# Pooled attention with a PReLU feed-forward net: the low bits of the weight words by ScalarE, pooling of two chunks by TensorE, a reordered first phase

## The chip, the cores and the metric

The kernel runs on one core of a Trainium2 chip. Its time is the device time of one execution in microseconds (us). Three timed runs of the kernel before gave a median of 908.95 us (908.25 to 910.93). The profile is of one more execution.

## The reference

```python
# attention: B, H, S, D = 8, 8, 576, 64, pool = 8; q and k carry a factor 8
k_p = k.reshape(B, H, S // 8, 8, D).mean(axis=3)
v_p = v.reshape(B, H, S // 8, 8, D).mean(axis=3)
scores = matmul(q, k_p.T) / sqrt(D)
attn = exp(scores - max(scores));  attn = attn / (sum(attn) + 1e-9)
x = matmul(attn, v_p)              # heads side by side: 4608 tokens x 512
# feed-forward: w_in 512 x 2048, w_out 2048 x 512, alpha per column of h
h = x @ w_in
g = maximum(h, 0) + alpha * minimum(h, 0)
out = g @ w_out
```

The two weight matrices arrive as words of 8 bytes (float64), everything else as float32.

## The kernel before

The 4608 tokens go in nine chunks of 512. A chunk needs the pooled keys and values of one or two batches, its scores, a softmax, the mixing product (`mix`, L543), and then the two feed-forward products: FFN1 (L671 to L673) in 16 steps of 128 columns of h, FFN2 (L717 to L719) in 16 steps that add one block of g each to the outputs of four token blocks. Every product runs in float16 pairs: a value is split into a high half and the rest, and each product is three matmuls (low by high, high by low, high by high). A FFN step for 512 tokens is so 12 matmuls. The splits need powers of two as scales, from maxima over partitions: `reduce_max` (L168 to L193) transposes the column of maxima on TensorE (L189), takes the maximum of each row on VectorE (L181), spreads it over a diagonal on VectorE (L182), sums the diagonal into all partitions on TensorE (L191) and clamps it on VectorE (L186).

The work has two phases. `start()` (L730 to L801) does chunk 0 wholly, the attention of chunk 1, and turns the weights into float16 pairs. A loop (L819 to L836) then goes over chunks 1 to 8 and lays the attention of the next chunk between the FFN1 steps of this one. The loop's text is the same before and after, except that it hands over the first chunk's g blocks by number instead of in a list.

The weight tiles are 128 partitions x 2 x 512 words: eight of w_in, eight of w_out. `convert` (L569 to L622) takes such a tile as pairs of 32-bit integers, `word(l, i, 1)` the high and `word(l, i, 0)` the low half of each word. ScalarE scales the high words as if they were float32 (L577 in two halves for w_in, L581 for w_out), which brings the exponent to the float32 place; VectorE shifts that left by three bits (L585), puts the top three bits of the low words under it (L587: shift right by 29, or), and puts the sign on (L590). ScalarE rounds to float16 (L601, L606), and the rest goes to VectorE or POOL: for w_in L620, every second tile on POOL, for w_out L609 on VectorE in 15 of 16 halves and otherwise L613 on ScalarE with L615 on POOL. Before all this VectorE takes the maxima of the raw tile (L210).

What waits for the weights: an FFN1 step needs its w_in block and x; its result is scaled out of PSUM by ScalarE (L677), goes through PReLU on VectorE (L681), is rounded by ScalarE (L688), and its rest is made by POOL (L691). An FFN2 step needs g, its w_out block, and, in `start()`, that all of FFN1 be scaled out, since its four accumulators (`acc`) take the PSUM of both. Idle stretches of TensorE are filled with matmuls whose result is not used (L739), in the first chunk only.

Keys and values of `start()` come in a transposed layout: k as 128 x 2304 (eight tokens of a window side by side), v as 72 x 4096. For chunk 0 VectorE sums the keys' windows (L308). For chunk 1 POOL does it in three halving steps (L303). POOL does the same for both chunks' values (L402). q is scaled to float16 by ScalarE (L370) and its rest made by VectorE (L382); one half of chunk 1's q goes over ScalarE and POOL instead (L376, L378).

The order of `start()` is worked out by a list scheduler when the kernel is built (`_Plan`, L61 to L115). Each operation carries an engine, an assumed cost, its predecessors, a rank, and buffers that it takes or gives. The scheduler goes forward in its own model time and lets each engine take, of the operations that are ready at about the same time, the one with the lowest rank. What results is a fixed instruction order for each engine: an engine executes its row in order, whatever is ready elsewhere. DMAs are issued by SyncE in such a row of its own.

## Time and profile before

| | us |
|---|---|
| median of three runs | 908.95 |
| the profiled execution | 907.43 |
| its span in the trace | 905.7 |
| TensorE busy in the span | 853.0 |
| VectorE busy | 447.2 |
| ScalarE busy | 398.0 |
| POOL busy | 394.0 |
| first FFN1 matmul of chunk 0 | at 56.11 |
| last conversion of a weight on VectorE ends | at 177.8 |
| first FFN1 matmul of chunk 1 | at 190.60 |

The span runs from the first to the last instruction that the trace holds; the profiled execution is 1.73 us longer. All times of a row are counted from the span's start. The granted TensorE clock was 0.975 of full speed in the mean. The stretch up to 190.6 us is `start()`, the rest the loop over chunks 1 to 8.

### The profile page before, as it was taken

To read this page: it belongs to the slowest core of one execution; us is meant where nothing else is said; L and a number is where in the kernel's file an instruction comes from. 1 tells how busy PE (TensorE), PEld (TensorE's weight loads), DVE (VectorE), ACT (ScalarE), POOL (GpSimd) and SP (SyncE) were. 2 spreads that over 40 slices of the span, in tenths; PEclk is the share of its full clock that TensorE was granted. 3 is DMA by queue.
4 is the path that set the end of the run, shared out by engine and by line. 5 is a ranking of instruction groups with operands and counts; after the bars stand their busy time and mean duration, and the time that the engine had idled before them with its cause. 6 is when DMAs were issued, how large, how long until landed. Compare 5 with 4: busy or idle time off the path is not lost.

```text
span 905.7 us, 11601 instructions
## 1 busy us (share of the span) xinstructions
PE 853.0 (94%) x4494; PEld 416.9 (46%) x4494; DVE 447.2 (49%) x733; ACT 398.0 (44%) x659; POOL 394.0 (43%) x386
## 2 busy tenths in 40 slices
PE   6587877889999999999999999999999999999998
PEld 5343343445444544454444444544454445444443
DVE  6999999746513651375137613641474136211110
ACT  3665565455632563256225522552354336323330
POOL 5539727635722572257125723471356027302320
PEclk8699998999999999999999999999999999999999
DMA  9791311550541054105410531063106102200000
GB/s 309 237 351 48 122 33 45 99 195 4 92 150 50 4 95 148 49 4 98 155 38 4 120 134 39 4 132 121 38 4 134 42 12 47 47 35 13 1 20 27
DMA packets 93015, 74.75 MB, mean 83 GB/s; under 512 B 77024, under 2 KB 77600, under 8 KB 92960
## 3 DMA queue, kind: packets, MB, share of 16 engines
q1 hardware_dynamic: 92960, 74.01, 29.0%
q8 instruction: 35, 0.57, 0.3%
q14 instruction: 20, 0.16, 0.1%
HBM read 45.10 MB, written 9.44 MB: 60 GB/s over the span
## 4 chain that ended last, share of the span: by engine, by line
PE 75%; DVE 15%; POOL 3%; DMA 2%; issue 2%; ACT 2%; SPq 1%; POOLq 0%; ACTq 0%; DVEq 0%
PE o L717 12%; PE o L719 12%; PE o L718 12%; PE h L671 11%; PE h L672 11%; PE h L673 11%; DVE v L587 2%; DVE v L590 2%; DVE m L210 2%; DMA qraw<-qT_dram 2%; DVE t L681 2%; DVE w L609 1%; PE x L543 1%; DVE v L585 1%; PE s L533 1%
## 5 line engine op out<-in xcount | busy, mean ns | idle before, releaser
L691 POOL TENSOR_TENSOR g<-t,g 128x512 f16<-128x512 f32 x144 | 178.9, 1246 | 312.5 <-ACT g L688 312.5
L681 DVE SCALAR_TENSOR_TENSOR t<-t,al 128x512 f32<-128x512 f32 x144 | 140.5, 976 | 251.0 <-ACT t L677 240.4
L671 PE MATMUL h<-x,w 128*128 128x512 f16 x576 | 219.8, 382 | 10.9 <-ACT t L677 8.1
L672 PE MATMUL h<-x,w 128*128 128x512 f16 x576 | 219.7, 381 | 1.2 <-DVE x L504 1.2
L673 PE MATMUL h<-x,w 128*128 128x512 f16 x576 | 219.3, 381 | 0.0
L718 PE MATMUL o<-w,g 128*128 128x512 f16 x544 | 207.1, 381 | 0.0
L717 PE MATMUL o<-w,g 128*128 128x512 f16 x544 | 205.9, 381 | 1.2 <-ACT o L707 1.2
L719 PE MATMUL o<-w,g 128*128 128x512 f16 x544 | 204.1, 381 | 0.0
L688 ACT CAST g<-t 128x512 f16<-128x512 f32 x144 | 88.7, 616 | 126.3 <-DVE t L681 126.0
L677 ACT ACTIVATE t<-h,rp 128x512 f32<-128x512 f32 x144 | 98.3, 683 | 84.8 <-PE h L673 79.1
L402 POOL TENSOR_TENSOR vraw<-vraw 72x512 f32<-72x512 f32 (+1 forms) x64 | 66.8, 1059 | 87.1 <-DMA vraw<-vT_dram 80.0
L672 PEld LDWEIGHTS <-w 128*128 128x128 f16 x576 | 56.6, 98 | 75.9 <-issue 14.0
L719 PEld LDWEIGHTS <-g 128*128 128x128 f16 x576 | 56.6, 98 | 69.0 <-issue 1.9
L673 PEld LDWEIGHTS <-w 128*128 128x128 f16 x576 | 56.6, 98 | 68.7 <-issue 3.1
L717 PEld LDWEIGHTS <-g 128*128 128x128 f16 x576 | 56.6, 98 | 68.5 <-issue 3.2
L718 PEld LDWEIGHTS <-g 128*128 128x128 f16 x576 | 56.7, 98 | 67.2 <-issue 2.6
L707 ACT ACTIVATE o<-o,os 128x512 f32<-128x512 f32 x34 | 22.6, 683 | 146.6 <-PE o L719 146.6
L671 PEld LDWEIGHTS <-w 128*128 128x128 f16 x576 | 56.6, 98 | 65.8 <-issue 2.0
L471 POOL TENSOR_TENSOR e<-e,sm 128x576 f32<-128x576 f32 x35 | 43.6, 1245 | 40.6 <-DVE sm L469 40.5
L504 DVE SCALAR_TENSOR_TENSOR x<-x,xsc,x 128x512 f16<-128x512 f32 x36 | 25.9, 747 | 70.1 <-ACT x L500 70.1
L476 ACT CAST apad<-e 128x576 f16<-128x576 f32 x72 | 44.9, 668 | 14.8 <-POOL e L471 13.9
L479 POOL TENSOR_TENSOR apad<-e,apad 128x448 f16<-128x448 f32 x36 | 42.9, 1191 | 13.9 <-ACT apad L476 13.9
(126 smaller groups left out, 849.9 us busy)
## 6 DMA issues: line engine op xcount, KB each, us to landing
w<-w_dram SPq DMA_DIRECT2D x16, 1024.0 KB
vraw<-vT_dram SPq DMA_DIRECT2D x32, 288.0 KB
out_dram<-o SPq DMA_DIRECT2D x36, 256.0 KB
qraw<-qT_dram SPq DMA_DIRECT2D x17, 512.0 KB
kraw<-kT_dram SPq DMA_DIRECT2D x14, 576.0 KB
kq<-kT_dram SPq DMA_DIRECT2D x2, 576.0 KB
aT<-apad SPq DMA_TRANSPOSE x36
kq<-qT_dram SPq DMA_DIRECT2D x1, 512.0 KB
```

The lines of the kernel that those rows point to most:

```text
L402: nc.gpsimd.tensor_tensor(out=o, in0=y, in1=z, op=ALU.add)
L476: x = add("ACT", 0.57, lambda l=l, ap=ap, ev_=ev_: nc.scalar.copy(out=ap[:, l, :, :SP], in_=ev_()), x, *td[i - 2:i - 1], rank=rk)
L671: nc.tensor.matmul(ps, w[:, 1, ks_], x[:, 0], start=(n == 0), stop=False)
L672: nc.tensor.matmul(ps, w[:, 0, ks_], x[:, 1], start=False, stop=False)
L673: nc.tensor.matmul(ps, w[:, 0, ks_], x[:, 0], start=False, stop=(n == NK - 1))
L677: nc.scalar.activation(t, hps.pop((c, f)), AF.Copy, scale=rp[:, f:f + 1])
L681: nc.vector.scalar_tensor_tensor(out=t, in0=t, scalar=al[:, f:f + 1], in1=t, op0=ALU.mult, op1=ALU.max)
L688: nc.scalar.copy(out=g[:, 0], in_=t)
L691: nc.gpsimd.tensor_tensor(out=g[:, 1], in0=t, in1=g[:, 0], op=ALU.subtract)
L717: nc.tensor.matmul(ps, g[:, 1, ts_], w[:, 0], start=(f == 0), stop=False)
L718: nc.tensor.matmul(ps, g[:, 0, ts_], w[:, 1], start=False, stop=False)
L719: nc.tensor.matmul(ps, g[:, 0, ts_], w[:, 0], start=False, stop=(f == NF - 1))
```

## The change

- The low words become small integers on ScalarE: in place, from unsigned 32-bit through a scale of 0.9365 x 2^-29 to a signed integer of 0 to 7 (L614 after). VectorE then shifts the scaled high word left by three and ors the small integer in one instruction (L628 after), and puts the sign on (L631 after). The shift of its own (L585) is gone, so a tile has two VectorE steps in place of three.
- Keys and values of chunks 0 and 1 arrive in their natural layout, 576 tokens by 512 (new inputs kN, vN), and TensorE pools them by a product with a window matrix of ones (`pooled`, L273 and L276 after, float32, five blocks of tokens; 20 matmuls for the keys, five for the values). ScalarE copies the result out of PSUM. L308, L402 and L303 are gone from `start()`. The rest of chunk 1's q is made by VectorE wholly.
- In `reduce_max` the diagonal moves from VectorE to ScalarE (L202 after).
- Of the 16 halves of w_out, ten instead of 15 have their rest made by VectorE; the other six go over ScalarE and POOL.
- The scheduler has other costs and ranks (`RK`), the maxima and the diagonal are operations of their own, and an FFN2 step may come as soon as all of FFN1 is scaled out, in any order that the ranks give.

```diff
+LOW3 = 0.9365 * 2.0 ** -29
...
+RK = dict(l1=257.15, step=3.65, l2=347.18, mx1=499.67, mx1s=-14.75, mx2=209.79, mx2s=20.58, grp=17.42,
...
-    HOP, DMA_HOP = 0.08, 2.0
+    HOP, DMA_HOP = 0.12, 2.0
...
+    pool = const.tile([P, SP + 4 * P // POOL], F32, name="pool")
+    nc.vector.memset(pool, 0.0)
+    w0 = 4 * P // POOL
+    nc.vector.memset(pool[:, w0:w0 + P // POOL], 1.0)
+    for k, b in ((1, 0), (-1, POOL - 1)):
+        nc.gpsimd.affine_select(out=pool[:, w0:w0 + P // POOL], in_=pool[:, w0:w0 + P // POOL], compare_op=ALU.is_ge,
+                                fill=0.0, base=b, pattern=[[-k * POOL, P // POOL]], channel_multiplier=k)
...
+        def maxima():
+            nc.vector.tensor_reduce(out=t()[:n], in_=ps()[:n, 0, :P], axis=AX.X, op=ALU.max)
+
         def diagonal():
-            nc.vector.tensor_reduce(out=t()[:n], in_=ps()[:n, 0, :P], axis=AX.X, op=ALU.max)
-            nc.vector.tensor_scalar(out=dg()[:n, :n], in0=ident[:n, :n], scalar1=t()[:n], scalar2=None, op0=ALU.mult)
+            nc.scalar.activation(dg()[:n, :n], ident[:n, :n], AF.Copy, scale=t()[:n])
...
-        x = add("DVE", 0.5, diagonal, x, rank=rank)
-        x = add("PE", 0.35, lambda: nc.tensor.matmul(ps()[:, 1, :n], ones[:n], dg()[:n, :n], start=True, stop=True),
+        x = add("DVE", 0.27, maxima, x, rank=rank)
+        x = add("ACT", 0.28, diagonal, x, rank=rank)
+        x = add("PE", 0.45, lambda: nc.tensor.matmul(ps()[:, 1, :n], ones[:n], dg()[:n, :n], start=True, stop=True),
...
+    def pooled(add, src, dst, rank, by_rows, behind=(), place=None):
+        t = place or big_tile([P, 4, DM], "nat")
+        u = once(lambda: fp.tile([P, DM], F32, tag="f", name="nat4"))
+        ps = once(lambda: ps_s.tile([P, 2, CH], F32, tag="s", name="pl"))
+        lds = []
+        for j in range(2):
+            lds += 2 * [load(add, lambda j=j: t()[:, 2 * j:2 * j + 2],
+                             src[2 * j * P:(2 * j + 2) * P].rearrange("(a p) n -> p a n", p=P), 1.6, rank,
+                             *behind, *lds[-1:], take=None if j else "aT" if place else "big")]
+        lds.append(load(add, lambda: u()[:S - 4 * P], src[4 * P:], 0.4, rank, lds[-1], take="f"))
+        def products(j):
+            rows, n = (t()[:, j], P) if j < 4 else (u(), S - 4 * P)
+            win = pool[:n, w0 - P // POOL * j:w0 - P // POOL * j + SP]
+            if by_rows:
+                nc.tensor.matmul(ps()[:SP, 0], win, rows[:n], start=(j == 0), stop=(j == 4))
+                return
+            for pp in range(NPR):
+                nc.tensor.matmul(ps()[:, 0, pp * SP:pp * SP + SP], rows[:n, pp * P:pp * P + P], win,
+                                 start=(j == 0 and pp == 0), stop=(j == 4 and pp == NPR - 1))
+        x = None
+        for j, ld in enumerate(lds):
+            x = add("PE", 0.95 if by_rows else 1.5, lambda j=j: products(j), ld, *([x] if x else []), rank=rank,
+                    take=None if j else "S", give=None if j < 4 else "f" if place else ("f", "big"))
+        if by_rows:
+            x = add("ACT", 0.69, lambda: nc.scalar.copy(
+                out=dst().rearrange("p h d -> p (h d)"), in_=ps()[:SP, 0]), x, rank=rank, take="f", give="S")
+        else:
+            x = add("ACT", 0.5, lambda: nc.scalar.copy(
+                out=dst().rearrange("p a s -> p (a s)"), in_=ps()[:, 0, :NPR * SP]), x, rank=rank, take="f", give="S")
+        return x, lds[0]
...
+                place = (lambda: qk()[:, 1].rearrange("p (a n) -> p a n", n=DM)) if early else None
+                kl[b] = pooled(add, kN[b], ks, rank, False, behind, place)
+                continue
...
-                if i < q_pool:
-                    h = add("ACT", 0.2 + 0.84 / q_cuts, lambda t=t, sc=sc, cs=cs: nc.scalar.activation(
-                        t()[:, :, cs], t()[:, :, cs], AF.Copy, scale=sc()), h, rank=rk)
-                    h = add("Pool", 0.1 + 2.0 / q_cuts, lambda q=q, t=t, cs=cs: nc.gpsimd.tensor_tensor(
-                        out=q()[:, 1, :, cs], in0=t()[:, :, cs], in1=q()[:, 0, :, cs], op=ALU.subtract),
-                        h, *h_after, rank=rk, **kw)
...
-            ps = []
+            ps = [pooled(add, vN[b], vs, rank + rks["v"], True, behind)[0]] if begin else []
...
+            low = add("ACT", 1.2, lambda: nc.scalar.activation(
+                word(l, i, 0).bitcast(I32), word(l, i, 0).bitcast(U32), AF.Copy, scale=LOW3), w_ld[l, i],
+                      rank=rank + RK[f"low{l}"])
...
-            x = add("DVE", 0.6, lambda: nc.vector.tensor_scalar(
-                out=vi(), in0=vi(), scalar1=3, scalar2=None, op0=ALU.logical_shift_left), x, rank=rank)
-            x = add("DVE", 1.13, lambda: nc.vector.scalar_tensor_tensor(
-                out=vi(), in0=word(l, i, 0).bitcast(I32), scalar=29, in1=vi(),
-                op0=ALU.logical_shift_right, op1=ALU.bitwise_or), x, rank=rank)
-            x = add("DVE", 1.13, lambda: nc.vector.scalar_tensor_tensor(
+            x = add("DVE", 1.3, lambda: nc.vector.scalar_tensor_tensor(
+                out=vi(), in0=vi(), scalar=3, in1=word(l, i, 0).bitcast(I32),
+                op0=ALU.logical_shift_left, op1=ALU.bitwise_or), x, low, rank=rank)
+            x = add("DVE", 1.4, lambda: nc.vector.scalar_tensor_tensor(
                 out=vi(), in0=word(l, i, 1).bitcast(I32), scalar=-2 ** 31, in1=vi(),
...
-                if picked(2 * i + j, 15):
-                    ys.append(add("DVE", 0.6, lambda j=j, sf=sf: nc.vector.scalar_tensor_tensor(
...
-        x = rd[-1]
+        x = rd
...
-            x = add("PE", 2.59, lambda f=f: step(f), gd[f], wd[2, f], x, rank=due[2](f))
-        attention(add, 1, [1], L2 + 0.62, early=True, k_pool=2, q_pool=1,
-                  on_act=(0, 1), behind=[ld[2, NF // 2 - 1]])
+            x = [add("PE", 2.59, lambda f=f: step(f), gd[f], wd[2, f], *x, rank=due[2](f))]
+        attention(add, 1, [1], L2 + RK["a1"], begin=True, on_act=(0, 1), behind=[ld[2, NF // 2 - 1]])
```

The first place is VectorE while it converts w_out, behind the middle of FFN1. `v` is the tile under conversion, `w` the raw tile with its number, `s` the scales, `t` an FFN1 result, `pt`, `pm`, `pr`, `e`, `wsc`, `w2s` and `w2e` the small tiles of a reduction or of the scales. Before:

```order
L587 SCALAR_TENSOR_TENSOR v<-w_629,v 128x1024
L585 TENSOR_SCALAR v<-v 128x1024
L590 SCALAR_TENSOR_TENSOR v<-w_629,v 128x1024
L587 SCALAR_TENSOR_TENSOR v<-w_651,v 128x1024
L585 TENSOR_SCALAR v<-v 128x1024
L590 SCALAR_TENSOR_TENSOR v<-w_651,v 128x1024
L587 SCALAR_TENSOR_TENSOR v<-w_682,v 128x1024
L655 SCALAR_TENSOR_TENSOR s_119<-e_116,w2s,sg 128x16
L590 SCALAR_TENSOR_TENSOR v<-w_682,v 128x1024
```

And after, the first tiles of w_out:

```order
L628 SCALAR_TENSOR_TENSOR v<-v,w_557 128x1024
L696 TENSOR_SCALAR w2e<-w2e 128x1
L725 SCALAR_TENSOR_TENSOR t<-t,al 128x512
L227 TENSOR_SCALAR w2s<-w2e 128x1
L631 SCALAR_TENSOR_TENSOR v<-w_557,v 128x1024
L699 SCALAR_TENSOR_TENSOR s_124<-e_121,w2s,sg 128x16
L725 SCALAR_TENSOR_TENSOR t<-t,al 128x512
L701 SCALAR_TENSOR_TENSOR wsc<-pa,w2e 128x1
L199 TENSOR_REDUCE pt<-pm 1x1
L628 SCALAR_TENSOR_TENSOR v<-v,w_589 128x1024
L628 SCALAR_TENSOR_TENSOR v<-v,w_609 128x1024
```

A tile has L628 and L631 where it had three instructions, the maximum of a reduction (L199) has no diagonal behind it, and the PReLU steps (L725) stand between the conversions.

The second place is ScalarE at the end of `start()`: `apad` is the last softmax piece of chunk 1, `x` its mixed values, `q` the next chunk's queries, `o` the outputs of chunk 0 in PSUM. Before:

```order
L476 CAST apad_97<-e 128x8x72 x2
L606 ACTIVATE w_809<-v,s_119 128x512
L500 ACTIVATE x_1626<-x,xsc 128x512
L500 ACTIVATE x_1628<-x,xsc 128x512
L500 ACTIVATE x_1643<-x,xsc 128x512
L500 ACTIVATE x_1646<-x,xsc 128x512
L314 ACTIVATE q_1721,m<-qraw 128x1024
L314 ACTIVATE q_1723,m<-qraw 128x1024
L707 ACTIVATE o<-h,os 128x512 x2
L707 ACTIVATE o<-o,os 128x512 x2
```

And after:

```order
L512 CAST apad_97<-e 128x8x72 x2
L751 ACTIVATE o<-h,os 128x512 x2
L536 ACTIVATE x_1535<-x,xsc 128x512
L536 ACTIVATE x_1538<-x,xsc 128x512
L358 ACTIVATE q_1611,m<-qraw 128x1024
L536 ACTIVATE x_1541<-x,xsc 128x512
L536 ACTIVATE x_1544<-x,xsc 128x512
L751 ACTIVATE o<-o,os 128x512 x2
L358 ACTIVATE q_1613,m<-qraw 128x1024
```

The outputs that free the PSUM of `h` stand ahead of the x pieces instead of behind both q pieces, and the second pair of x pieces stands behind the first q piece.

The third place is the row of DMA issues of SyncE at the program's start: `kraw` and `nat` are keys in the old and the new layout, `w` a tile of w_in. Before:

```order
L222 DMA kraw<-kT_dram 128x1152 x2
L222 DMA qraw<-qT_dram 128x1024
L222 DMA al<-al_dram 128x16
L222 DMA vraw<-vT_dram 72x1024 x2
L222 DMA w_138<-w_dram 128x2x1024
L222 DMA qraw<-qT_dram 128x1024
```

And after:

```order
L243 DMA nat<-kN_dram 128x2x512
L243 DMA w_131<-w_dram 128x2x1024
L243 DMA nat<-kN_dram 128x2x512
L243 DMA w_150<-w_dram 128x2x1024
L243 DMA nat_164<-kN_dram 64x512
L243 DMA qraw<-qT_dram 128x1024
```

Two tiles of w_in stand between the key loads now, ahead of the queries; the first values are loaded further back.

## Rows read from the trace of the kernel before

**Rows 1.** The page: shares of the chain that ended last, by engine.
```profile
PE 75%; DVE 15%; POOL 3%; DMA 2%; issue 2%; ACT 2%; SPq 1%; POOLq 0%; ACTq 0%; DVEq 0%
```
**Rows 2.** Windows: stretch, length, busy us of each engine, clock, DMA share, GB/s.
```profile
0.00:56.90 56.90, 35.92 (x247) 27.79 (x248) 47.42 (x99) 29.57 (x67) 29.30 (x40) 0.79 0.91 280
56.90:124.50 67.60, 52.59 (x244) 24.42 (x244) 65.96 (x69) 36.87 (x56) 46.54 (x28) 0.94 0.35 129
124.50:177.80 53.30, 47.13 (x245) 22.80 (x244) 50.81 (x74) 33.40 (x71) 33.17 (x32) 0.91 0.24 54
177.80:190.60 12.80, 7.30 (x49) 3.46 (x47) 3.27 (x9) 5.45 (x10) 0.28 (x1) 0.87 0.87 261
190.60:905.70 715.10, 710.08 (x3712) 338.42 (x3711) 279.79 (x486) 292.74 (x459) 284.66 (x287) 1.00 0.23 61
```
**Rows 3.** VectorE's groups, 0 to 178 us: line, shape, count, busy us, mean ns.
```profile
L590 DVE SCALAR_TENSOR_TENSOR v<-w,v 128x1024 int32<-128x1024 int32 x16 | 25.9, 1620 | 0.0
L587 DVE SCALAR_TENSOR_TENSOR v<-w,v 128x1024 int32<-128x1024 int32 x16 | 23.5, 1469 | 0.1
L210 DVE TENSOR_REDUCE m<-w 128x2 f32<-128x1024 f32 x16 | 19.1, 1203 | 0.0
L609 DVE SCALAR_TENSOR_TENSOR w<-v,s,w 128x512 f16<-128x512 f32 x15 | 14.8, 1006 | 1.8 <-ACT w L606 1.8
L585 DVE TENSOR_SCALAR v<-v 128x1024 int32<-128x1024 int32 x16 | 14.0, 876 | 0.0
L182 DVE TENSOR_SCALAR pd<-ident,pt 1x1 f32<-1x1 f32 (+4 forms) x12 | 6.6, 554 | 0.5
...
L382 DVE SCALAR_TENSOR_TENSOR q<-qraw,s,q 128x512 f16<-128x512 f32 (+1 forms) x5 | 4.6, 954 | 0.9 <-ACT q L370 0.9
```
**Rows 4.** Single VectorE lines, 0 to 180 us: ns shortest/median/longest, first and last start.
```profile
L590 DVE SCALAR_TENSOR_TENSOR v<-w,v x16: 1208/1214/4252, 33.5 to 173.2; 128x1024 int32<-128x1024 int32 x16
...
L210 DVE TENSOR_REDUCE m<-w x16: 1161/1206/1214, 16.0 to 104.2; 128x2 f32<-128x1024 f32 x16
```
**Rows 5.** POOL's groups, 0 to 178 us.
```profile
L691 POOL TENSOR_TENSOR g<-t,g 128x512 f16<-128x512 f32 x16 | 24.3, 1527 | 11.8 <-ACT g L688 11.8
L402 POOL TENSOR_TENSOR vraw<-vraw 72x512 f32<-72x512 f32 (+1 forms) x16 | 20.0, 1248 | 19.1 <-DMA vraw<-vT_dram 18.5
...
L402 POOL TENSOR_TENSOR vs<-vraw 72x128 f32<-72x128 f32 x8 | 5.8, 735 | 0.5
L303 POOL TENSOR_TENSOR kq<-kq 128x576 f32<-128x576 f32 (+1 forms) x4 | 5.0, 1259 | 0.0
...
L378 POOL TENSOR_TENSOR q<-kq,q 128x1024 f16<-128x1024 f32 x1 | 2.1, 2115 | 0.0
```
**Rows 6.** ScalarE's groups, 0 to 178 us.
```profile
L456 ACT ACTIVATE e<-s,nb,ds 128x72 f32<-128x72 f32 x32 | 12.6, 423 | 5.6 <-DVE ds L519 3.4 <-DVE nb L450 1.7 <-DVE sm L469 0.6
...
L581 ACT ACTIVATE v<-w 128x1024 f32<-128x1024 f32 x8 | 8.9, 1150 | 0.0
...
L613 ACT ACTIVATE v<-v,s 128x512 f32<-128x512 f32 x1 | 0.7, 722 | 0.0
```
**Rows 7.** TensorE's groups of small float32 products, 0 to 190.6 us.
```profile
L189 PE MATMUL pm<-ident,m 128*2 128x128 f32 (+4 forms) x9 | 2.6, 293 | 7.8 <-DVE m L210 3.7 <-DVE rp L631 2.3 <-ACT q L314 1.4
```
**Rows 8.** The chain that ended last, around 190 us: start, us, what.
```profile
181.27 7.54 DMA qraw<-qT_dram
...
189.98 0.58 ACT o L707
190.60 0.38 PE h L671
190.98 0.22 PE h L672
```
**Rows 9.** ScalarE's first wait for queries: start, us, what, idle before.
```profile
7.67 1.06 ACT L314 ACTIVATE q<-qraw 128x1024 f16<-128x1024 f32 x1 [5.66 <-DMA qraw<-qT_dram]
```
**Rows 10.** The page: DMA issues of the weights, size of each.
```profile
w<-w_dram SPq DMA_DIRECT2D x16, 1024.0 KB
```

More of the change, by code (lines that the diff above doesn't have):

```diff
@@ L111, in emit @@
                 self.room[op["take"]].remove(min(self.room[op["take"]]))
-            if op["give"]:
-                self.room[op["give"]].append(op["end"])
+            for kind in op["give"]:
+                self.room[kind].append(op["end"])
             op["emit"]()
@@ L247, in attention @@
         first = c == 0
+        early = begin and not first
+        rks = {n: RK[n + str(min(c, 1))] for n in ("q", "v", "sm", "sms", "mix")}
         if early:
-            kq = once(lambda: atp.tile([P, NPR * S + NPR * HC], F32, tag="aT", name="kq"))
-        kl = {}
+            qk = once(lambda: atp.tile([P, 2, 4 * DM], F32, tag="aT", name="qk"))
+        kl, kss = {}, {}
         for b in bs:
+            ks = kss[b] = once(lambda: fp.tile([P, NPR, SP], F32, tag="f", name="ks"))
             kl[b] = []
+            if begin:
+                place = (lambda: qk()[:, 1].rearrange("p (a n) -> p a n", n=DM)) if early else None
+                kl[b] = pooled(add, kN[b], ks, rank, False, behind, place)
+                continue
@@ L278, in attention @@
             vl[b] = []
-            for i in range(4):
+            for i in range(0 if begin else 4):
                 if i % 2 == 0:
@@ L554, in load_w @@
         if wide:
-            return load(add, lambda: t().bitcast(I32), src.bitcast(I32), 2.92, rank, *after, take="big")
-        return load(add, lambda: t()[:, :, :512], src, 1.46, rank, *after, take="big")
+            w_ld[l, i] = load(add, lambda: t().bitcast(I32), src.bitcast(I32), 2.92, rank, *after, take="big")
+        else:
+            w_ld[l, i] = load(add, lambda: t()[:, :, :512], src, 1.46, rank, *after, take="big")
+        return w_ld[l, i]
     def word(l, i, n):
@@ L600, in convert @@
         if l == 1:
-            x = add("ACT", 0.95, lambda: nc.scalar.copy(out=part(0), in_=v()), x, rank=rank)
+            x = add("ACT", 1.05, lambda: nc.scalar.copy(out=part(0), in_=v()), x, *free, rank=rank)
         else:
```

199 lines of the change are left out of this document (95 added, 104 removed).

## Prediction

> **What bounds the kernel now.** I read the windows by stage first, then VectorE's groups, then POOL and ScalarE, then the end of the chain. The windows [rows 2] split the span at 190.60 us, where chunk 1's FFN1 begins. After that TensorE is busy 710.08 of 715.10 us at clock 1.00: nothing there depends on the change, and I leave it at 715.1. All that can move lies in the first 190.6 us. There VectorE is the full engine: 65.96 of 67.60 us between 56.9 and 124.5, 50.81 of 53.30 after that. TensorE is busy 52.59 and 47.13 there, at clocks of 0.94 and 0.91. The chain's 15% for VectorE [rows 1] is 136 of 905.7 us, the same stretch seen from the other side. From 177.8 on neither works: 12.8 us pass over the last transposes, the next queries' transfer of 7.54 us, and the outputs that ScalarE takes out behind it [rows 8].
>
> So an us taken from VectorE between about 14 and 178 us is an us off the end, until another engine is as late. I count by VectorE first, then ask who is next.
>
> **Off VectorE.** The shift L585 is 16 x 0.876 = 14.0 us [rows 3], all in the full stretch: -14.0. Its two partners keep form and count; L628 reads two inputs as L587 did, so I cost the exchange at nothing. The diagonal L182 is 12 x 0.554 = 6.6; two of the twelve (estimate 0.7) fall before 14 us, where VectorE has gaps: -5.9. Five of the 15 halves L609 go: 5 x 1.006 = -5.0. A half of chunk 1's q comes back from POOL: L382's mean of 0.954 is mostly for half that size, twice that is 1.9: +1.9. The k sum L308 goes too, but it stands in the first 8 us, where VectorE waits for transfers: 0. Sum: -23.0.
>
> **Off POOL.** Gone are the values' halving steps of both chunks (20.0 + 5.8), the keys' of chunk 1 (5.0) and L378 (2.1): 32.9 us [rows 5]. Five halves come, at most 5 x 1.527 (L691's mean, same shape) = 7.6. Net -25, about half of it after 56.9 us, since chunk 0's values, some 13 us, are pooled earlier. POOL itself has room in every window [rows 2], so this pays only through VectorE: L590 takes 1.208 at its shortest, 1.620 in the mean and once 4.252, whereas the maxima L210, with one input, stay between 1.161 and 1.214 [rows 3, 4]. Something stretches two-input steps, and POOL is the neighbour that works then. L590 lies 16 x 0.412 = 6.6 us above that shortest in all and L587, of the same form, 16 x 0.261 = 4.2: 10.8 us, against 109 us of POOL's work up to 177.8. In proportion, 25 us less of it are 10.8 x 25/109 = 2.5 on these two lines alone. Ends: 0, if the remaining POOL steps only meet other partners, and -25, if each POOL us had blocked VectorE wholly. I take -3.2, near what the rows measure, with a little for the other two-input lines.
>
> The Trainium skill ("SBUF — State Buffer", section "Who interferes with whom") calls the port pair that VectorE shares with GpSimd an exclusive lock, held for a whole instruction; reductions don't want it. The two lines [rows 4] agree in kind. By a full lock the term would be up to -25 and not -3.2; the mean of 1.620 against 1.208 speaks for a partial overlap.
>
> **Onto ScalarE.** The low words: 16 steps of 128x1024, read and written in place at a stride of two words. No row has the integer form. Nearest is L581, the same words' high halves to float32, at 1.150 [rows 6]: 18.4 us. Ends: 0.72 x 16 = 11.5 (as if half the size, L613) and 3 us each = 48 (above POOL's slowest group of that size, L378 at 2.115). I take 18.4, since shape and stride are L581's. The diagonals: 12 x 0.423 at most (L456) = 5.1; five w_out halves: 5 x 0.722 (L613) = 3.6; four copies out of PSUM at about the same = 2.9. Together +30 on the 99.8 that ScalarE is busy up to 177.8 [rows 2]: 130 of some 160 us. There is room in the sum, but ScalarE stands in order between VectorE's steps (scale, round) and between FFN1 and PReLU. Each of the 16 low steps can hold up something that VectorE or TensorE waits for. Ends: 0 and all 30. I take +5, about a third of a low step each time: until now ScalarE is busy 36.87 + 33.40 of the 120.9 us after 56.9 [rows 2], so 42% idle, and the planner's order puts lows, which need only their load, into gaps.
>
> A rule against that exchange stands in the Trainium skill ("ScalarE: Activation LUTs", section "Rules for kernel authors"): simple arithmetic belongs on VectorE, up to about three times as fast there. The rows agree in direction: 14.0 us leave VectorE for 18.4 on ScalarE. Were ScalarE the full engine, the change would lose 4.4; that is the second rival's ground.
>
> **TensorE's pooling.** 25 float32 products per chunk. Nearest is L189, float32 with 128 columns at 0.293 [rows 7]: by columns (20 of 72, 5 of 512) 3.3 + 5.9 = 9.2, by count 7.3. Ends 5 and 18, should such a product take twice as long as L189 shows. Chunk 0's lie where TensorE only idles with fill. Chunk 1's stand between FFN steps; TensorE waits there anyway for VectorE, for 67.60 - 52.59 = 15 us alone, and I take +2 on the path.
>
> **The begin.** Ahead of the first queries two w_in tiles are now loaded, 2.1 MB [rows 10], where ScalarE first waits until 7.67 us [rows 9]. At the 280 GB/s of the window [rows 2] that is up to 7.5 us more for the queries. VectorE uses the time: the raw maxima (1.2 us each, the first at 16.0 before [rows 4]) come earlier, and VectorE had 9.5 us free before 56.9. I take +2 (ends -3 and +7.5).
>
> **The tail.** TensorE waited until 190.60 for the output evacuation L707, which stood behind both q pieces; now `h` is freed ahead of x. Saved: the 1.8 us from the landing of the queries at 181.27 + 7.54 = 188.81 to 190.60 [rows 8], more if x alone had been earlier. But the second pair of x stands behind the first q piece, so the next transfer still counts. I take -1 (ends -4 and +3).
>
> **Sum.** -23.0 - 3.2 + 5 + 2 + 2 - 1 = -18.2. On the profiled execution's 907.43: 889.2; the median is 1.5 above that, so 908.95 - 18.2 = 890.8. I say 890.5. Chunk 1's FFN1 would begin at 172.4 us. Check by TensorE: after 56.9 it had 52.59 + 47.13 + 7.30 = 107.0 us of work, plus about 7 of pooling: 56.9 + 2 + 107 + 7 = 172.9. So by then TensorE is nearly full as well, and no larger gain on VectorE would show.
>
> **Rivals.** First, TensorE runs clean. 538 matmuls after 56.9 at the 710.08/3712 = 0.191 us of the loop [rows 2] are 102.9 instead of 107.0; with pooling at 5 and FFN1 beginning no later, chunk 1 begins at 165: -26, 883. For it: VectorE's relief could be far over 3. Against: the pooling, and 16 FFN1 steps that each still wait on ScalarE and VectorE.
>
> Second, ScalarE's row becomes the bound: its 30 us count half, +15 instead of +5, and the relief falls to 0: -5 to -8, about 902. For it: no engine gets as much added. Against: the 42% idle.
>
> Third, slower: the in-place integer step is dear. Up to 177.8 ScalarE has 99.8 + 30 - 18.4 = 111.4 without it, and from 7.67 us some 170 us of time: it becomes the bound from (170 - 111.4)/16 = 3.7 us a step. At 4.5 us it ends at 7.7 + 111.4 + 72 = 191, 13 us behind VectorE's old end of 177.8: 922. For it: no row shows such a conversion. Against: every ScalarE group of this size is at 1.05 to 1.15.
>
> Fourth, the gain doesn't arrive: the queries' late landing holds x of chunk 0 up by the whole 7.5, the pooling stands in FFN1's way with 7 us and the order adds waits of ScalarE's for 5 more: -23 + 19.5 = -3.5, about 905.5, or less.
>
> **How the numbers follow.** Forecast 0.45 (884 to 898), clean TensorE 0.24, ScalarE's row 0.17, slower 0.07, no gain 0.07. What a measurement of this kernel can tell from no change is about 0.3%, or 2.7 us: 906.2 to 911.7. Faster: the first three whole (0.86) and a third of the fourth, 0.88; same: 0.05; slower: 0.07. The range for 8 in 10 leaves out the slower case, the no-gain case and the outer ends of the first: 875 to 904. The low end is TensorE clean and FFN1 begun 8 us earlier.
>
> **What would show it.** In the new profile: the loop from chunk 1's FFN1 on at 715; two VectorE instructions of 1.2 to 1.6 us per tile; the integer step at about 1.15 on ScalarE; L631's mean nearer its shortest than 1.620 is to 1.208; TensorE busy over 90% between the first FFN1 step and chunk 1's. The forecast is wrong if the integer step is over 2 us, if x of chunk 0 comes after 62 us, or if TensorE waits on ScalarE between FFN1 steps for more than some 10 us.

## The result

The changed kernel takes 896.63 us (median of 4 runs, 895.87 to 897.66) against 909.77 of the kernel before in the same series: a ratio of 0.9857 (95% interval 0.9837 to 0.9877), 13.1 us less. The forecast was 890.5 with a range of 875 to 904: right in direction, 6.1 us too low.

The windows of the profile after, cut about where the stages of [rows 2] end (first FFN1 of chunk 0, first FFN2 step, VectorE's last step of the first phase, first FFN1 of chunk 1), and once more two FFN1 steps later; columns as there:

```profile
0.00:59.30 59.30, 38.64 (x202) 27.94 (x202) 43.43 (x94) 43.02 (x88) 25.53 (x31) 0.88 0.78 256
59.30:115.08 55.78, 49.28 (x242) 24.36 (x240) 53.85 (x59) 44.45 (x66) 42.20 (x23) 0.96 0.45 171
115.08:163.30 48.22, 48.22 (x245) 22.41 (x245) 38.60 (x60) 34.99 (x74) 19.64 (x22) 0.95 0.26 58
163.30:170.10 6.80, 6.80 (x55) 3.14 (x54) 0.02 (x1) 2.12 (x4) 0.40 (x2) 1.00 0.85 208
170.10:182.06 11.96, 7.52 (x27) 2.78 (x25) 4.75 (x6) 5.72 (x11) 3.64 (x4) 0.86 0.76 257
182.06:894.70 712.64, 705.48 (x3688) 336.05 (x3687) 276.01 (x465) 294.33 (x475) 285.00 (x283) 1.00 0.23 60
```

Chunk 1's FFN1 begins at 170.10 instead of 190.60: the first phase is 20.5 us shorter. VectorE is still full during FFN1 (53.85 of 55.78), but from 115.08 on TensorE is, without a gap (48.22 of 48.22). Then comes what the forecast has no term for: the fifth row, 24 matmuls of FFN1 that take 11.96 us. In the profile of before the same 24 took 5.18 (190.60 to 195.78). Of the 6.8 us between them TensorE stands still for 4.4 (11.96 - 7.52); the other 2.3 are busy time (7.52 for 5.18), at a granted clock of 0.86 in the mean instead of 1.00.

VectorE's groups up to 163.3 us, the answer to [rows 3]; and the PReLU line of before, which was not shown there:

```profile
L631 DVE SCALAR_TENSOR_TENSOR v<-w,v 128x1024 int32<-128x1024 int32 x16 | 23.9, 1491 | 0.0
L725 DVE SCALAR_TENSOR_TENSOR t<-t,al 128x512 f32<-128x512 f32 x16 | 23.0, 1439 | 1.3 <-ACT t L721 1.2
L628 DVE SCALAR_TENSOR_TENSOR v<-v,w 128x1024 int32<-128x1024 int32 x16 | 20.8, 1306 | 0.0
...
L653 DVE SCALAR_TENSOR_TENSOR w<-v,s,w 128x512 f16<-128x512 f32 x10 | 9.1, 926 | 0.0
```

```profile
L681 DVE SCALAR_TENSOR_TENSOR t<-t,al 128x512 f32<-128x512 f32 x16 | 18.3, 1141 | 1.5 <-ACT t L677 1.3
```

Both conversion steps are shorter than in [rows 3], by 2.0 and 2.7 us in all, and the PReLU step is longer, by 4.7. In these three lines the stretch of VectorE's two-input steps has moved from one to the other and has not shrunk. ScalarE's two new groups, and TensorE's pooling products, in the same stretch:

```profile
L614 ACT ACTIVATE w<-w 128x1024 int32<-128x1024 uint32 x16 | 18.1, 1137 | 6.7 <-DMA w<-w_dram 6.7
...
L202 ACT ACTIVATE pd<-ident,pt 1x1 f32<-1x1 f32 (+4 forms) x12 | 3.4, 290 | 4.2 <-DVE pt L199 4.2
```

```profile
L276 PE MATMUL pl<-pool,nat 128*128 128x72 f32 (+1 forms) x48 | 10.3, 396 | 0.0
L273 PE MATMUL pl<-nat,pool 128*72 128x512 f32 (+1 forms) x20 | 10.0, 600 | 0.4 <-DMA nat<-vN_dram 0.4
...
L276 PE MATMUL pl<-pool,qk 128*128 128x72 f32 x32 | 3.9, 270 | 0.0
```

The integer step costs 1.137 us, as a float step of that shape does [rows 6]. The profile counts two matmuls for a float32 product (50 products, 100 records).

### The profile page after: what moved, and what is told of

Read it like the earlier page. It is cut to its first block, busy times and chain, and to the rows that moved or that the text cites. A ratio compares the mean times of both kernels' runs of the same rounds, so it can differ in the third digit from the quotient of the medians.

```text
span 894.7 us, 11495 instructions
## 1 busy us (share of the span) xinstructions
PE 855.9 (96%) x4451; PEld 416.7 (47%) x4451; DVE 416.7 (47%) x681; ACT 424.6 (47%) x715; POOL 376.4 (42%) x362
## 4 chain that ended last, share of the span: by engine, by line
PE 79%; DVE 8%; ACT 4%; DMA 4%; POOL 3%; issue 2%; SPq 1%; POOLq 0%; ACTq 0%; DVEq 0%
PE o L761 12%; PE o L762 12%; PE o L763 12%; PE h L715 12%; PE h L716 12%; PE h L717 12%; DVE t L725 3%; DMA qraw<-qT_dram 3%; PE x L579 1%; PE s L568 1%; PE s L570 1%; PE s L569 1%; PE pl L276 1%; DVE v L631 1%; DVE m L231 1%
## 5 line engine op out<-in xcount | busy, mean ns | idle before, releaser
L735 POOL TENSOR_TENSOR g<-t,g 128x512 f16<-128x512 f32 x144 | 177.1, 1233 | 312.6 <-ACT g L732 285.9
L725 DVE SCALAR_TENSOR_TENSOR t<-t,al 128x512 f32<-128x512 f32 x144 | 144.5, 1004 | 252.2 <-ACT t L721 246.7
L751 ACT ACTIVATE o<-o,os 128x512 f32<-128x512 f32 x34 | 22.6, 682 | 145.0 <-PE o L763 145.0
L438 POOL TENSOR_TENSOR vraw<-vraw 72x512 f32<-72x512 f32 (+1 forms) x48 | 46.8, 996 | 77.4 <-DMA vraw<-vT_dram 67.1
```

Source lines behind the costliest of these rows:

```text
L438: nc.gpsimd.tensor_tensor(out=o, in0=y, in1=z, op=ALU.add)
L725: nc.vector.scalar_tensor_tensor(out=t, in0=t, scalar=al[:, f:f + 1], in1=t, op0=ALU.mult, op1=ALU.max)
L735: nc.gpsimd.tensor_tensor(out=g[:, 1], in0=t, in1=g[:, 0], op=ALU.subtract)
```

## The experiments

All times are medians; in the table the stages come from the profiled execution of each kernel (us from the span's start). The kernels were measured in several series, each beside the kernel before, so differences of 1 or 2 us between two rows are best read by their ratios and intervals. "Chunk 1" runs from its first FFN1 matmul to its last FFN2 matmul, "rest" from there to the end of the span.

| kernel | FFN1 of chunk 0 | first FFN2 | FFN1 of chunk 1 | chunk 1 | rest | median | ratio to before (95%) |
|---|---|---|---|---|---|---|---|
| before | 56.1 | 124.2 | 190.6 | 89.9 | 625.2 | 909.8 | 1 |
| after | 59.3 | 111.6 | 170.1 | 97.0 | 627.6 | 896.6 | 0.9857 (0.9837 to 0.9877) |
| x_before_q | 60.4 | 112.3 | 169.5 | 96.7 | 627.2 | 895.6 | 0.9834 (0.9805 to 0.9863) |
| q_behind_t | 59.8 | 111.6 | 169.9 | 93.9 | 631.0 | 895.2 | 0.9831 (0.9802 to 0.9860) |
| own_out_buffers | 59.3 | 111.6 | 170.2 | 93.6 | 627.9 | 892.7 | 0.9814 (0.9785 to 0.9844) |
| loads_earlier | 59.3 | 111.1 | 172.1 | 91.3 | 630.2 | 896.2 | 0.9857 (0.9823 to 0.9890) |
| kq_early_own_buffers | 59.3 | 111.0 | 169.3 | 90.4 | 628.3 | 889.8 | 0.9782 (0.9757 to 0.9808) |
| low_on_dve | 64.2 | 121.7 | 191.9 | 92.2 | 627.0 | 914.4 | 1.0049 (1.0028 to 1.0071) |
| only_low | 59.3 | 121.5 | 185.4 | 91.9 | 624.9 | 903.4 | 0.9926 (0.9903 to 0.9948) |
| low_twice | 66.2 | 118.1 | 183.6 | 92.4 | 629.2 | 906.2 | 0.9968 (0.9953 to 0.9984) |
| pool_chunk1_back | 59.3 | 110.5 | 182.9 | 92.0 | 630.8 | 909.2 | 0.9986 (0.9967 to 1.0006) |
| diag_and_halves_back | 62.9 | 120.5 | 184.4 | 92.8 | 627.5 | 910.8 | 1.0002 (0.9982 to 1.0022) |
| all_parts_undone | 86.8 | 131.7 | 202.0 | 93.1 | 627.4 | 924.3 | 1.0159 (1.0128 to 1.0191) |
| no_g_rest | 59.2 | 107.3 | 160.8 | 96.8 | 630.1 | 891.8 | 0.9796 (0.9757 to 0.9835) |

### Where the 7 us of chunk 1 went

ScalarE's timeline of the kernel after at that place (start, us, what, idle before and what ended it), and TensorE's:

```profile
174.68 1.06 ACT L358 ACTIVATE q<-qraw 128x1024 f16<-128x1024 f32 x1 [4.10 <-DMA qraw<-qT_dram]
...
175.74 1.25 ACT L536 ACTIVATE x<-x,xsc 128x512 f16<-128x512 f32 x2
...
181.32 1.28 ACT L721 ACTIVATE t<-h,rp 128x512 f32<-128x512 f32 x2 [2.14 <-issue]
```

```profile
176.46 0.59 PE L715 MATMUL h<-x,w 128*128 128x512 f16 x2 [2.72 <-ACT x L536]
...
182.06 0.38 PE L715 MATMUL h<-x,w 128*128 128x512 f16 x1 [0.23 <-ACT t L721]
```

The second pair of x pieces (175.74) stands behind a query piece that waits for its transfer until 174.68, and TensorE waits for x. The obvious reading is ScalarE's order, and **x_before_q** and **q_behind_t** test it. The edit of x_before_q, cut:

```diff
+                    last["xa"] = nc.scalar.activation(x()[:, 0], ps()[:, k], AF.Copy, scale=xsc)
...
-            with tc.issue_after(last["t"].ins), tc.issue_after(last["x"].ins):
+            with ExitStack() as behind:
+                for k in ("t", "x", *(("xa",) if c == 1 else ())):
+                    behind.enter_context(tc.issue_after(last[k].ins))
```

`xa` is the last x piece on ScalarE; q_behind_t has `("xa", "sc", "g")`, with the latest FFN1 result on ScalarE and the latest g piece on POOL.

Expected of x_before_q:

> The changed kernel (896.63 us), except that on ScalarE the next chunk's two query pieces stand behind all four x pieces of chunk 1 instead of behind the second. Theory A: chunk 1's FFN1 begins 20.5 us earlier than before, and 6.8 of these are lost in its first 24 matmuls because ScalarE's row holds x behind a query transfer that lands at 174.7 us, and TensorE then runs at its lower clock. By A the idle 2.7 us and the slow matmuls behind it go, but the FFN1 results still stand behind the query pieces: -3 us, about 893.5. Theory B: the transfers for chunk 2 (queries, then values for POOL) end last anyway, and what is won here is waited for a few steps later: within 1 us of 896.6.

Expected of q_behind_t:

> As the one with x ahead of the queries, and in chunk 1 also the attention work of chunk 2 on ScalarE and POOL stands behind the FFN1 result (ScalarE) and the g piece (POOL) of the step with which it is issued, so that neither a query piece nor a value sum that waits for its transfer holds a FFN1 step up. Theory A (order on ScalarE and POOL, not the transfer): all 6.8 us come back, about 890. Theory B: chunk 2's attention, now later, becomes late for chunk 2 itself and the gain is paid back at the end of chunk 1: 894 or more.

Both stand 1.0 and 1.5 us below the kernel after (895.6 and 895.2), with overlapping intervals: the theory of the order falls as the main cause. In q_behind_t chunk 1 itself took 3.1 us less than in the kernel after, and the rest 3.4 more, so its theory B was right that the gain is paid back, if somewhat later than it said. What the order hid was another wait. ScalarE's first FFN1 result of chunk 1 in x_before_q, SyncE's issues beside it, and the same result in q_behind_t:

```profile
178.64 1.31 ACT L722 ACTIVATE t<-h,rp 128x512 f32<-128x512 f32 x2 [1.33 <-DMA out_dram<-o]
```

```profile
169.31 3.39 SPq L757 DMA_DIRECT2D out_dram<-o  x4
181.23 0.75 SPq L243 DMA_DIRECT2D vraw<-vT_dram  x2
```

```profile
178.75 1.30 ACT L722 ACTIVATE t<-h,rp 128x512 f32<-128x512 f32 x2 [6.02 <-DMA out_dram<-o]
```

With x and the queries out of its way, the result still starts at 178.7, now waiting for a store. Chunk 0's four outputs take all four buffers that FFN1 results and key sums also use, and their stores are issued behind 2.75 MB of loads for chunk 2. **own_out_buffers** gives the outputs other buffers, on top of x_before_q (cut to what it adds to that):

```diff
-        o = fp.tile([P, DM], F32, tag="f", name="o")
+        if c:
+            o = fp.tile([P, DM], F32, tag="f", name="o")
+        else:
+            if i % 2 == 0:
+                oss["first"] = wp.tile([P, 2, 512], F32, tag="v", name="o0", bufs=ROOM["v"])
+            o = oss["first"][:, i % 2]
```

> As the one with x ahead of the queries (895.6 us), and chunk 0's four output tiles have two buffers of their own (those of the weight conversion, free by then) instead of the four buffers that the FFN1 results, key sums and output tiles share. Theory C, from the trace of that kernel: the first FFN1 result of chunk 1 waits until 178.64 us for an output's store, the stores stand in the DMA queues behind 2.75 MB of loads for chunk 2, and by the same buffers the key sums and, behind them, the second pair of value loads (issued at 181.2) are late, so that POOL's first g comes at 187.8. By C most of this goes: FFN1 results from 177.3 (then the queries hold them), value loads some 5 us earlier: 889 to 892. Rival D: transfers are what is short, not buffers; with other buffers the same loads land at the same times: 894.5 or more.

892.7, 2.9 less than with x ahead alone, just above what theory C expected (the runs of the two don't overlap, the intervals of their ratios do). The store's wait is gone; what is left are the queries and, on POOL, values:

```profile
177.07 1.25 ACT L722 ACTIVATE t<-h,rp 128x512 f32<-128x512 f32 x2
```

```profile
182.95 2.50 POOL L438 TENSOR_TENSOR vraw<-vraw 72x512 f32<-72x512 f32 x2 [0.38 <-DMA vraw<-vT_dram]
185.41 1.15 POOL L736 TENSOR_TENSOR g<-t,g 128x512 f16<-128x512 f32 x1
```

**loads_earlier** takes the other half of the story, the loads, with the old buffers, also on top of x_before_q (cut):

```diff
...
-            with tc.issue_after(last["t"].ins), tc.issue_after(last["x"].ins):
+            with ExitStack() as behind:
+                for k in (("x", "xa") if c == 1 else ("t", "x")):
+                    behind.enter_context(tc.issue_after(last[k].ins))
```

`t` is the last transpose, behind which chunk 2's loads no longer stand.

> As the one with x ahead of the queries (895.6 us), and the key, query and first value loads of chunk 2 are issued ahead of chunk 1's last softmax transposes instead of behind them (row order of SyncE alone; buffers as before). Theory C (chunk 0's stores and chunk 2's loads come together at 165 to 178 us): queries have landed when ScalarE reaches them, the stores find empty queues and land some 6 us sooner, FFN1 results are free to go by 174: 888 to 891. Rival: the loads delay the transposes that they are issued ahead of, and the mixing product of chunk 1 comes later by what is won: 895 or more.

896.2: nothing. The rival was right, with a twist: the values now stand in the way of the transposes on POOL. A value sum waits in POOL's row ahead of the last softmax piece, and the mixing product waits for that:

```profile
161.85 2.49 POOL L438 TENSOR_TENSOR vraw<-vraw 72x512 f32<-72x512 f32 x2 [1.92 <-DMA vraw<-vT_dram]
164.30 1.03 POOL L515 TENSOR_TENSOR apad<-e,apad 128x448 f16<-128x448 f32 x1
```

Against x_before_q, chunk 1 itself took 91.3 instead of 96.7, but began 2.6 us later, and the rest took 3.0 more. So **kq_early_own_buffers** moves keys and queries ahead (the four operations of `line.emit(4)`) and leaves the values behind the transposes, with x ahead and the outputs' own buffers (cut):

```diff
...
+                if c == 1 and f == 0:
+                    line.emit(4)
+                behind.enter_context(tc.issue_after(last["t"].ins))
```

> Three changes to the end of the first phase of the changed kernel together: x ahead of the queries on ScalarE, two buffers of their own for chunk 0's outputs, and chunk 2's keys and queries (not its values) loaded ahead of chunk 1's softmax transposes. Theory C in full (queue, buffers and order at 165 to 180 us cost chunk 1 some 7 us): with the outputs' own buffers alone FFN1 results still waited for the queries until 177.1 us and POOL's first g until 185.4; with the queries there, results go from 173.5 and the values land some 4 us sooner: 888 to 890. Rival: as with all loads ahead of the transposes (896.2), loads in that place push the transposes back, and nothing comes on top of 892.7.

889.8 (888.68 to 893.31, 6 runs), as expected; it beats both kernels, and chunk 1 takes 90.4 us, nearly the 89.9 of before. The result starts as soon as its product is there, and POOL's first g comes 9.3 us earlier than in the kernel after (188.69 there):

```profile
175.13 1.26 ACT L722 ACTIVATE t<-h,rp 128x512 f32<-128x512 f32 x2 [0.97 <-PE h L718]
```

```profile
179.38 1.15 POOL L736 TENSOR_TENSOR g<-t,g 128x512 f16<-128x512 f32 x1
```

That settles the 7 us of chunk 1: queries, stores and values come together at the first phase's end. x ahead alone brought 1 us, the outputs' own buffers on top of it 2.9, the earlier keys and queries on top of both another 2.9. Own buffers or earlier keys and queries without x ahead were not run.

### What the parts are worth

**low_on_dve** has the three-step form of before in `convert`, and no integer step (cut):

```diff
-            low = add("ACT", 1.2, lambda: nc.scalar.activation(
...
+            x = add("DVE", 0.8, lambda: nc.vector.tensor_scalar(
+                out=vi(), in0=vi(), scalar1=3, scalar2=None, op0=ALU.logical_shift_left), x, rank=rank)
...
-                out=vi(), in0=vi(), scalar=3, in1=word(l, i, 0).bitcast(I32),
-                op0=ALU.logical_shift_left, op1=ALU.bitwise_or), x, low, rank=rank)
+                out=vi(), in0=word(l, i, 0).bitcast(I32), scalar=29, in1=vi(),
+                op0=ALU.logical_shift_right, op1=ALU.bitwise_or), x, rank=rank)
```

> The changed kernel with the low words back on VectorE: no integer step on ScalarE, and a shift of its own on VectorE, three VectorE steps per weight tile as before. The prediction's term: each of the 16 shifts of 0.88 us lies on the path, +14 us, about 910. Rival: since the change TensorE is full from 115 us on (48.2 of 48.2 us), so that only the shifts that fall before that count, about ten of 16: +7 to +9, about 904. Second rival, by the order on ScalarE: 18 us less on ScalarE give most of it back: +3 or less.

914.4, +17.8, more than the 14.5 us that the 16 shifts take in that trace, although 18.1 us leave ScalarE. So it is neither rival, and it is more than the shifts can explain: the order, made for two steps, adds waits of its own. That TensorE is full after 115 us saves nothing here: its next blocks are then late enough that TensorE waits for w_out's, 3.8 us for POOL and 3.4 for VectorE. Chunk 1's FFN1 begins 21.8 us later, and chunk 1, which now begins 13.8 us behind its first load, gives 4.8 back. **only_low** is the kernel before with the integer step (ranked like its tile's conversion) and two VectorE steps, in effect the reverse of that diff:

> The kernel before (909.5 us) with one part of the change alone: low words become small integers on ScalarE, two VectorE steps per tile; pooling, diagonals, the ranks and costs stay as before. Prediction's terms for this part: -14.0 on VectorE and +5 of ScalarE: -9, about 900.5. Rival: without the reordering the added ScalarE steps stand in the way in the old order, which was made for fewer of them: within 3 us of before. Second rival, all 14 us: 895.

903.4, -6: between the forecast's 900.5 and the first rival. Of the 14.0 us that leave VectorE, 8 come back. It is the one part that was measured by itself in an order that was not made for the whole. **low_twice** adds a second integer step on ScalarE:

```diff
+            low = add("ACT", 1.2, lambda: nc.scalar.activation(
+                word(l, i, 0).bitcast(I32), word(l, i, 0).bitcast(I32), AF.Copy, scale=1.0), low,
+                      rank=rank + RK[f"low{l}"])
```

> The changed kernel with a second integer step on ScalarE for each low word tile (integers 0 to 7 to themselves, 1.14 us each, 16 of them, which VectorE waits for). It measures what an us more on ScalarE costs: the prediction took a third of a low step, so +5 to +6 us, 902. Rival, ScalarE with room to spare (it is busy 122 of the first 163 us): +2 or less, 898. Rival, ScalarE as the bound: +12 or more, 909.

906.2, +9.5 for 18.3 us of ScalarE: half of each us shows in the time. FFN1 of chunk 0 began 6.9 us later and that of chunk 1 13.5, of which chunk 1 gave 4.6 back (92.4 for 97.0). Chunk 1 gives 4 to 5 us back in all kernels of this section that are made from the one after and start it later. At the end of the first phase chunk 1's mixing product waited for the last softmax transposes:

```profile
180.29 3.35 PE L579 MATMUL x<-aT,v 88*64 88x448 f16 x28 [7.24 <-DMA aT<-apad]
```

**pool_chunk1_back** takes, for chunk 1, the path that later chunks take:

```diff
-        attention(add, 1, [1], L2 + RK["a1"], begin=True, on_act=(0, 1), behind=[ld[2, NF // 2 - 1]])
+        attention(add, 1, [1], L2 + RK["a1"], begin=False, on_act=(0, 1), behind=[ld[2, NF // 2 - 1]])
```

> The changed kernel with the pooling of chunk 1 (not chunk 0) off TensorE: keys summed by VectorE (2 x 1.35 us) from the transposed layout, values by POOL in halving steps (about 13 to 16 us). The prediction's terms (TensorE's pooling costs 2, VectorE relief 3 in all, 1.5 of it here): within 2 us of 896.6, slightly slower. Rival 1: TensorE is full behind 115 us, so that the 5 us of value products there and 4 us of key products come off the path: 888 to 892. Rival 2: POOL's steps hold up VectorE's two-input steps and the values come late for the mixing product: +5 or more, 902.

909.2, +12.5: the second rival, and far from the forecast's 2. Again it is the softmax that is late:

```profile
179.45 3.52 PE L579 MATMUL x<-aT,v 88*64 88x448 f16 x28 [8.41 <-DMA aT<-apad]
```

**diag_and_halves_back** undoes two small parts (cut):

```diff
-            nc.scalar.activation(dg()[:n, :n], ident[:n, :n], AF.Copy, scale=t()[:n])
+            nc.vector.tensor_scalar(out=dg()[:n, :n], in0=ident[:n, :n], scalar1=t()[:n], scalar2=None, op0=ALU.mult)
...
-        x = add("ACT", 0.28, diagonal, x, rank=rank)
+        x = add("DVE", 0.28, diagonal, x, rank=rank)
...
-                if picked(2 * i + j, 10):
+                if picked(2 * i + j, 15):
```

> The changed kernel (896.6 us) with the diagonals of the reductions back on VectorE and 15 instead of ten halves of w_out's rest there. The prediction's terms: 5.9 + 5.0 on VectorE less about a third of the 8.7 us that ScalarE is rid of: +8, about 904.5. Rival: behind 115 us TensorE is full and VectorE has 9.6 us free, so the halves, which all lie there, cost nothing and the diagonals only what lies before: +2 to +4, about 899.5.

910.8, +14.1 instead of +8. **all_parts_undone** has the edits of low_on_dve and diag_and_halves_back, and `begin=False` for both chunks:

> The changed kernel's ranks, costs and edges, with the work of before: shift on VectorE, keys and values summed by VectorE and POOL in both chunks (all keys by VectorE, all of q's rest by VectorE), diagonals on VectorE, 15 halves of w_out's rest on VectorE. Theory A: the gain comes from the work moved, the order only serves it: slower than before, since VectorE has 2.7 + 1.9 us more than before and the ranks were for other work: 915 to 930. Rival: the new order alone brings part of the gain: under 906.

924.3, in the range of theory A: the new ranks without the moved work lose 14.5 us against before. This run mixes two things, though. Its first FFN1 step comes at 86.8 us, 27.5 later than in the kernel after, while the kernel before, with the same work, is there at 56.1: the ranks fit the old work badly, above all at the start. Taken back one at a time, three parts cost 17.8, 12.5 and 14.1, 44.4 in all; taken back together (with chunk 0's pooling too) they cost 27.7. The order was worked out for all of them, so a single part taken back costs its own time and what the order then puts in its way. I read these figures as bounds from above for a part's worth. No part but the integer step was run in an order that was not made for the whole, so how the 13.1 us divide between the moved work and the new order stays open.

**no_g_rest** leaves the rest of g out in chunk 0: POOL fills the low halves with zeros:

```diff
-            nc.gpsimd.tensor_tensor(out=g[:, 1], in0=t, in1=g[:, 0], op=ALU.subtract)
+            if c:
+                nc.gpsimd.tensor_tensor(out=g[:, 1], in0=t, in1=g[:, 0], op=ALU.subtract)
+            else:
+                nc.gpsimd.memset(g[:, 1], 0.0)
```

> The changed kernel (896.6 us) with POOL's rest of g in chunk 0 left out: a fill with zeros stands in its place, in the same order, so that POOL reads nothing there and works some 20 us less while VectorE is full (the low halves of chunk 0's g are missing in the result). It measures what POOL's work costs VectorE. Between 59 and 115 us the PReLU steps take 1.44 us in the mean and 0.74 at the shortest, 11 us over in all, the two conversion steps 2.6 us over. By the prediction's average (10.8 us of stretch to 109 us of POOL): -2, about 894.5. By the share of that stretch (13.8 us to 42.2 us of POOL): -6.5, 890. Rival, a full lock: all 11 us of the PReLU steps and what waits on them go: -11, 885.5. Second rival, TensorE is the bound there already: within 1 us.

891.8 (888.76 to 894.77), -4.8; chunk 1's FFN1 began 9.3 us earlier, of which the profiled execution keeps 7.0. The measured -4.8 lies between the forecast's average and the share of the stretch. The PReLU line (shortest/median/longest ns) of the kernel before, of the kernel after and of this one:

```profile
L681 DVE SCALAR_TENSOR_TENSOR t<-t,al x16: 736/888/2608, 63.3 to 124.5; 128x512 f32<-128x512 f32 x16
```

```profile
L725 DVE SCALAR_TENSOR_TENSOR t<-t,al x16: 737/1496/2616, 64.2 to 107.9; 128x512 f32<-128x512 f32 x16
```

```profile
L725 DVE SCALAR_TENSOR_TENSOR t<-t,al x16: 739/752/2393, 63.5 to 103.9; 128x512 f32<-128x512 f32 x16
```

POOL's 16 steps went from 24.9 to 7.8 us. VectorE's busy time up to 163 us went from 135.9 to 129.7, of which 1.4 are chunk 1's x pieces that the kernel after makes only later: 7.6 us less for the same work, 0.44 us of VectorE for an us of POOL. It goes the other way too: POOL's rests of the weights (L664 and L659) fell from 31.5 to 26.8 us. In the kernel after one of them takes 5.43 us, and TensorE waits for it at the first FFN2 step:

```profile
115.08 0.58 PE L762 MATMUL o<-w,g 128*128 128x512 f16 x1 [3.14 <-POOL w L659]
```

The matmuls behind that wait stood 0.43 us apart instead of 0.22 up to 119.7; in no_g_rest the wait is 0.52 us and the granted clock stays at 1.00. This is part of why the first phase kept 9.3 us, more than VectorE's 7.6.

## Why the prediction was right in sign and 6 us off

**The step that failed** is the first: "nothing there depends on the change, and I leave it at 715.1". Chunk 1's FFN1 began earlier than forecast (170.10 instead of 172.4), but from there to the end the profiled execution took 724.6 us, 9.5 more: 7.1 in chunk 1 and 2.4 behind it. The forecast saw the second pair of x behind a query piece, and priced the whole tail at -1 (ends -4 and +3). It missed that the loads of chunk 2, the stores of chunk 0 and the values for POOL are issued in one heap when the first phase ends. SyncE issues the first of these loads at (after, then before):

```profile
165.67 1.51 SPq L243 DMA_DIRECT2D kraw<-kT_dram  x2
```

```profile
179.26 1.49 SPq L222 DMA_DIRECT2D kraw<-kT_dram  x2
```

So the loads moved 13.6 us ahead and FFN1 20.5: it began 11.3 us behind the first load before (the queries had landed at 188.81, [rows 8]) and begins 4.4 us behind it now. These 6.9 us are about what chunk 1 loses, but the head start is not all of it: in low_twice and pool_chunk1_back FFN1 begins 4.9 and 5.1 us behind the first load, and chunk 1 takes only 92.4 and 92.0 us. There chunk 0's stores are issued ahead of the loads (from 172.97 and 171.49, the loads from 178.69 and 177.81), and not behind them as in the kernel after (stores from 169.71). With the three edits of kq_early_own_buffers, 6.6 of the 7.1 us come back in chunk 1, and 6.8 in the median.

Part of the early begin is where the cut lies. From VectorE's last step of the first phase to chunk 1's FFN1 it was 12.8 us before (177.8 to 190.6) and is 6.8 now (163.3 to 170.1), because FFN1 now starts on the first two of four x pieces. To the 25th matmul of that FFN1 it was 18.0 and is 18.8. Counted so, VectorE's last step came 14.5 us earlier (forecast 17.2), the tail cost 0.8 (forecast -1), and what is behind it 2.7 (forecast 0): 11.0 in the profiled execution, 13.1 in the medians. The forecast's sentence that "neither works" in the 12.8 us was a misreading too: TensorE is busy for 7.30 of them [rows 2].

The 2.4 us in the rest are of the same kind. TensorE waits there for the outputs that ScalarE takes out of PSUM, 2.4 us in the kernel after and 0.4 before (the waits of TensorE behind chunk 1: us in all, times, longest; after, then before):

```profile
PE o L761 <- ACT o L751: 2.4, 3, 1.6
```

```profile
PE o L717 <- ACT o L707: 0.4, 2, 0.3
```

At the longest of these waits the outputs stand on ScalarE behind a query piece whose transfer is late:

```profile
516.48 1.06 ACT L358 ACTIVATE q<-qraw 128x1024 f16<-128x1024 f32 x1 [0.79 <-DMA qraw<-qT_dram]
...
517.53 1.25 ACT L751 ACTIVATE o<-o,os 128x512 f32<-128x512 f32 x2
```

Over all kernels of the table this wait goes from 0.2 us (only_low, rest 624.9) to 5.1 (loads_earlier, rest 630.2), and the rest without it lies between 624.7 and 627.0. Why the queries land later from one kernel to the next is open.

**VectorE's terms**: the work left as forecast, and a little more. VectorE is busy 135.9 us up to 163.3 against 164.2 up to 177.8 [rows 2], 28.3 less: the shift 14.0, the diagonals 6.6, the halves of w_out 5.7 and the key sums 2.7, against 0.9 more for q. But an us off VectorE was not an us off the end. Its last step came 14.5 us earlier, because its idle time up to there grew by 13.8 us: by 6.4 in the first stage and by 7.1 after 115 us, where TensorE is the full engine. The forecast's +5, +2 and +2 for ScalarE, pooling and the begin are 9.

**The relief by POOL** of 3.2 us did not come. POOL lost 21.6 us (109.0 to 87.4 up to the same places) and the conversion steps got 4.7 us shorter, but the PReLU step got 4.7 longer: its median is 888 ns before and 1496 after. What counts is which POOL step runs beside which VectorE step, and not the sum of POOL's time. The rows of before showed the stretch of the PReLU line, which I left out (18.3 us against 16 x 0.74). no_g_rest shows that POOL's step is what stretches most of it. The Trainium skill ("SBUF — State Buffer", section "Who interferes with whom") says that a VectorE step with two inputs from SBUF contends with a GpSimd instruction that reads SBUF and not with one that only writes it. The PReLU step agrees: its median falls from 1496 to 752 ns when POOL's step only writes.

**ScalarE's term** had durations near the forecast (18.1 us of low words, forecast 18.4; +22.6 us in all, forecast +30) and too low a price: I had taken a sixth of the 30, while low_twice shows 0.52 us per us and only_low 8 us for 18. At 0.52 the +22.6 would be +11.8 and not +5. That is an estimate, since no run takes ScalarE's part alone out of the new order. That the sum came within 6 us is in part luck: 2.1 us more than forecast left VectorE, while the waits set against that were 4.8 too low.

**TensorE's pooling** takes 10.2 us of busy time for chunk 1 (5.2 for the values, 5.0 for the keys): inside the ends of the estimate of 9.2. As the forecast's check said, TensorE was nearly full by then, in truth full from 115 us. Moving that work back off TensorE cost 12.5, far more than the 2 that it was priced at; it puts 13.7 us of value sums on POOL and 2.7 of key sums on VectorE in that trace.

**The begin** cost 3.2 us (59.3 for 56.1), forecast +2, though not by the queries alone. SyncE issues the last piece of chunk 0's values behind a transpose that waits for the softmax, and the mixing product waits for what follows from them:

```profile
36.42 1.96 SPq L523 DMA_TRANSPOSE aT<-apad  x1
38.43 1.07 SPq L243 DMA_DIRECT2D nat<-vN_dram  x1
```

```profile
55.73 3.63 PE L579 MATMUL x<-aT,v 88*64 88x512 f16 x16 [1.18 <-DMA v<-v]
```

The same product before:

```profile
54.24 1.94 PE L543 MATMUL x<-aT,v 88*64 88x512 f16 x16 [1.17 <-DMA aT<-apad]
```

It starts 1.5 us later and takes 1.7 us longer, at a granted clock of 0.50 in place of 1.00: in the kernel before it follows unused matmuls (L739) that end 1.2 us ahead of it, while in the kernel after TensorE has little to do just ahead of it (busy for 1.27 of the 6.70 us from 49.0 on).

Of the rivals, TensorE running clean is half true (full from 115 us on, but FFN1's stretch still waits for VectorE), the dear integer step fell (1.137 us), and ScalarE's row as the bound was right in its price (about half) and in its relief of 0, though not in the sum.

## What to carry to other kernels

A stage that "does not depend on the change" depends on when it starts: look at what transfers, stores and buffers the earlier start will meet, and follow the shared buffers to whoever frees them last. Where three things wait at one place, removing one can move the wait to the next, so test them together as well as apart. A sum of an engine's time does not price what it does to its neighbour; look at which steps run side by side. In an order that was worked out for a set of edits, taking one edit back measures the edit and the misfit together.
